# PSUM banks handed on to other tiles, a new order of the first products, and dense dummy products during the loads, in a gated mix of linear attention and SwiGLU

## The chip, the cores and the metric

The kernel runs on one core of one Trainium2 chip. The metric is the time of one execution in microseconds (us), taken on the device. Every time quoted is of a fast run; no run in this study was of the slow state. The engines are called as the profile calls them: PE (TensorE), DVE (VectorE), ACT (ScalarE), POOL (GpSimd), SP (SyncE, which here only issues transfers).

## The reference, cut to what matters

```python
x = A_x                                           # 1 x 2048 x 512, bf16
g = sigmoid((x * gate_w).sum(-1, keepdims=True))
# A: linear attention, 32 heads of 16
q, k, v = split(x @ wqkv)
pq, pk = phi(q), phi(k)                           # phi(t) = where(t > 0, t + 1, exp(t)) + 1e-6
kv  = einsum("bhsd,bhse->bhde", pk, v)            # sums over ALL tokens
z   = einsum("bhsd->bhd", pk)
a   = (einsum(pq, kv) / (einsum(pq, z) + 1e-6)) @ wo
# B: SwiGLU
b   = (silu(x @ w1) * (x @ w3)) @ w2              # F = 1376
return g * a + (1 - g) * b
```

The sums over all tokens come first. The kernel does not form v: it accumulates XP = x^T pk over the 16 token tiles of 128 tokens in four PSUM banks (XP0 to XP3), and multiplies by the weights of v afterwards. So the program begins with: load x and the key weights, transpose x, k = x wk, pk = phi(k), XP += x^T pk.

## The kernel before

The kernel keeps eight buffers in PSUM, each of up to 128 x 512 fp32, which are called banks here. Four (`psM`, tag "mm") rotate. The other four belong to three pools one after another: first the keys of token tiles 0 to 3, then the XP accumulators, then two output and two query buffers.

```python
psM = tile_pool(name="psM", bufs=4, space=PSUM)
...
def phi(dst, ps):                                 # one key or query tile, 128 x 512
    e  = exp(ps)                                  # ACT
    em = min(e, 1.0) + 1e-6                       # DVE, phi_m
    dst = max(ps, 0.0) + em                       # DVE, the last reader of the bank
...
warm = psM.tile([P, P], FP32, tag="mm", name="warm")
for i in range(18):                               # 18 dummy products of 128 columns
    nc.tensor.matmul(warm[:], lhsT=zeros[:], rhs=zeros[:], start=True, stop=True)
mask_ps = psM.tile([P, P], FP32, tag="mm", name="mask_ps")
nc.tensor.matmul(mask_ps[:], lhsT=EhT[:], rhs=EhT[:], start=True, stop=True)
nc.vector.tensor_copy(out=blockmask[:], in_=mask_ps[:])
...
def emit_xT(t):                                   # transposes token tile t on PE
    xTp = psM.tile([P, KC, P], BF16, tag="mm", name="xTp")
    ...                                           # 4 transposes, then a copy by DVE or ACT
...
with tc.tile_pool(name="psE", bufs=1, space=PSUM) as psE:
    k0 = [psE.tile([P, D], FP32, tag=f"k{t}", name=f"k0_{t}") for t in range(TPB)]
    emit_xT(0)
    emit_k_mm(k0[0], 0, 0)                        # key tile 0, contraction chunk 0 of 4
    emit_xT(1)
    emit_k_mm(k0[0], 0, 1)
    emit_k_mm(k0[1], 1, 0)
    emit_xT(2)
    ...                                           # the rest, then the last chunk of each:
    for t in range(TPB):
        emit_k_mm(k0[t], t, 3)
        emit_k_phi(k0[t], t)

with tc.tile_pool(name="psX", bufs=1, space=PSUM) as psX:      # the four banks of psE again
    XP_ps = [psX.tile([P, D], FP32, tag=f"XP{dc}", name=f"XP{dc}") for dc in range(KC)]
    for t in range(TPB, NT):
        emit_k(t)                                 # 4 products, bank from psM
        emit_xp(...)                              # 4 products, one into each XP bank
    ...
psO = tile_pool(name="psO", bufs=2, space=PSUM)   # and these again the same four
psQ = tile_pool(name="psQ", bufs=2, space=PSUM)
```

The order of instructions on PE is the order of the program; the other engines are ordered by the framework.

Of the kernel before, what the change touches and what calls it, by code (L numbers as in the profile page):

```python
# [8 lines left out]
ACT = mybir.ActivationFunctionType  # L9
# [3 lines left out]
FP32 = mybir.dt.float32  # L13
BF16 = mybir.dt.bfloat16
# [3 lines left out]
def kernel(  # L18
# [12 lines left out]
    nc = tc.nc  # L31
    P = nc.NUM_PARTITIONS

    Bb, S, D = A_x.shape
# [3 lines left out]
    KC = D // P  # L38
    NT = S // P
    TB = 512  # L40
    NTB = S // TB
    TPB = TB // P
# [9 lines left out]
    consts = ctx.enter_context(tc.tile_pool(name="consts", bufs=1))  # L52
    work = ctx.enter_context(tc.tile_pool(name="work", bufs=3))
    blk = ctx.enter_context(tc.tile_pool(name="blk", bufs=2))
    psM = ctx.enter_context(tc.tile_pool(name="psM", bufs=4, space=bass.MemoryType.PSUM))


    zeros = consts.tile([P, P], BF16, name="zeros")
    nc.vector.memset(zeros[:], 0.0)
    ident = consts.tile([P, P], BF16, name="ident")  # L60
    make_identity(nc, ident[:])
# [3 lines left out]
        out=EhT[:], in_=EhT[:], pattern=[[1, P]], compare_op=ALU.is_ge, fill=0.0,  # L65
# [3 lines left out]
        out=EhT[:], in_=EhT[:], pattern=[[-1, P]], compare_op=ALU.is_ge, fill=0.0,  # L69
# [32 lines left out]
    for tb in range(1, NTB):  # L102
        dq.dma_start(
            out=xT[:, :, tb * TB : (tb + 1) * TB], in_=x2d[tb * TB : (tb + 1) * TB, :],
# [3 lines left out]
            out=x_sb[:, tb * TPB : (tb + 1) * TPB, :], in_=x_r[:, tb * TPB : (tb + 1) * TPB, :]  # L108
# [4 lines left out]
    with nc.allow_non_contiguous_dma(reason="one gate weight per partition and chunk"):  # L113
        dq.dma_start(
            out=wr_sb[:, :, 2 * FR : NR], in_=gate_w.rearrange("(kc d o) -> d kc o", d=P, o=1)
# [11 lines left out]
    XP_sb = consts.tile([P, KC, D], BF16, name="XP_sb")  # L127
# [22 lines left out]
    ctx.enter_context(tc.manual_schedule(engines={ENG.PE}))  # L150


    warm = psM.tile([P, P], FP32, tag="mm", name="warm")
    for i in range(18):
        nc.tensor.matmul(warm[:], lhsT=zeros[:], rhs=zeros[:], start=True, stop=True)
    mask_ps = psM.tile([P, P], FP32, tag="mm", name="mask_ps")
    nc.tensor.matmul(mask_ps[:], lhsT=EhT[:], rhs=EhT[:], start=True, stop=True)
    nc.vector.tensor_copy(out=blockmask[:], in_=mask_ps[:])

    st = {}  # L160

    def emit_xT(t):
        xTp = psM.tile([P, KC, P], BF16, tag="mm", name="xTp")
        for kc in range(KC):
            nc.tensor.transpose(
                out=xTp[:, kc, :], in_=x_sb[:, t, kc * P : (kc + 1) * P], identity=ident[:]
            )
        xT_t = xT[:, :, t * P : (t + 1) * P]
        if t % 2 == 0:
            nc.vector.tensor_copy(out=xT_t, in_=xTp[:])  # L170
        else:
            nc.scalar.activation(out=xT_t, in_=xTp[:], func=ACT.Copy)

    def emit_k_mm(k_ps, t, kc):
        nc.tensor.matmul(  # L175
            k_ps[:], lhsT=xT[:, kc, t * P : (t + 1) * P], rhs=wk_sb[:, kc, :],
            start=(kc == 0), stop=(kc == KC - 1),
        )

    def emit_k_phi(k_ps, t):  # L180
        e_ins = phi(pk_sb[:, t, :], k_ps[:])
        if t == 0:
            nc.gpsimd.tensor_copy(pks[:], pk_sb[:, t, :])
        else:
            nc.gpsimd.tensor_add(pks[:], pks[:], pk_sb[:, t, :])  # L185

    def emit_k(t):
        k_ps = psM.tile([P, D], FP32, tag="mm", name="k_ps")
        for kc in range(KC):
            emit_k_mm(k_ps, t, kc)  # L190
        emit_k_phi(k_ps, t)

    def emit_xp(t, XP_ps):
        for dc in range(KC):
            nc.tensor.matmul(  # L195
                XP_ps[dc][:], lhsT=x_sb[:, t, dc * P : (dc + 1) * P], rhs=pk_sb[:, t, :],
                start=(t == 0), stop=(t == NT - 1),
            )

    def emit_q(tb, tt, pool, tag):  # L200
        t = tb * TPB + tt
        ts_tok = slice(t * P, (t + 1) * P)
        if tt == 0:
            st[tb, "pq"] = blk.tile([P, TPB, D], BF16, tag="pq", name="pq")
            st[tb, "den"] = blk.tile([P, TPB, H], FP32, tag="den", name="den")
        q_ps = pool.tile([P, D], FP32, tag=tag, name="q_ps")
        for kc in range(KC):
            nc.tensor.matmul(  # L208
                q_ps[:], lhsT=xT[:, kc, ts_tok], rhs=wq_sb[:, kc, :],
                start=(kc == 0), stop=(kc == KC - 1),  # L210
            )
        phi(st[tb, "pq"][:, tt, :], q_ps[:])
# [105 lines left out]
    def emit_out(tb, tt):  # L318
        t = tb * TPB + tt
        tsl = slice(tt * P, (tt + 1) * P)  # L320
        o_ps = psO.tile([P, D], FP32, tag="o", name="o_ps")
        for c in range(KC):
            nc.tensor.matmul(  # L323
                o_ps[:], lhsT=st[tb, "pqT"][:, c, tsl], rhs=W_sb[:, c, :],
                start=(c == 0), stop=False,
            )
        nc.tensor.matmul(  # L327
            o_ps[:], lhsT=st[tb, "hTr"][:FR, tsl], rhs=w2r_sb[:FR, :], start=False, stop=False
        )
        for fc in range(FC):  # L330
            nc.tensor.matmul(  # L331
                o_ps[:], lhsT=st[tb, "hT"][:, fc, tsl], rhs=w2_sb[:, fc, :],
                start=False, stop=(fc == FC - 1),
            )
        o_out = work.tile([P, D], BF16, tag="o_out", name="o_out")
        nc.scalar.activation(  # L336
            out=o_out[:], in_=o_ps[:], func=ACT.Copy, scale=omg[:, t : t + 1]
        )
        nc.sync.dma_start(out=out2d[t * P : (t + 1) * P, :], in_=o_out[:])


    with tc.tile_pool(name="psE", bufs=1, space=bass.MemoryType.PSUM) as psE:
        k0 = [psE.tile([P, D], FP32, tag=f"k{t}", name=f"k0_{t}") for t in range(TPB)]
        emit_xT(0)
        emit_k_mm(k0[0], 0, 0)
        emit_xT(1)
        emit_k_mm(k0[0], 0, 1)
        emit_k_mm(k0[1], 1, 0)
        emit_xT(2)
        emit_k_mm(k0[1], 1, 1)  # L350
        emit_k_mm(k0[0], 0, 2)
        emit_k_mm(k0[1], 1, 2)
        emit_xT(3)
        for kc in range(KC - 1):
            emit_k_mm(k0[2], 2, kc)
        for kc in range(KC - 1):
            emit_k_mm(k0[3], 3, kc)
        for t in range(TPB):
            emit_k_mm(k0[t], t, 3)
            emit_k_phi(k0[t], t)  # L360


    with tc.tile_pool(name="psX", bufs=1, space=bass.MemoryType.PSUM) as psX:
        XP_ps = [psX.tile([P, D], FP32, tag=f"XP{dc}", name=f"XP{dc}") for dc in range(KC)]
        n_xp = 0
        for t in range(TPB, NT):
            emit_k(t)
            for u in range(n_xp, n_xp + (2 if t in (NT - 4, NT - 2) else 1)):
                emit_xp(u, XP_ps)
                n_xp = u + 1  # L370
        emit_q(0, 0, psM, "mm")
        emit_xp(NT - 2, XP_ps)
        emit_q(0, 1, psM, "mm")
        emit_xp(NT - 1, XP_ps)
        for dc in range(KC):
            if dc % 2 == 0:
                nc.scalar.activation(out=XP_sb[:, dc, :], in_=XP_ps[dc][:], func=ACT.Copy)
            else:
                nc.vector.tensor_copy(out=XP_sb[:, dc, :], in_=XP_ps[dc][:])

    psO = ctx.enter_context(tc.tile_pool(name="psO", bufs=2, space=bass.MemoryType.PSUM))
    psQ = ctx.enter_context(tc.tile_pool(name="psQ", bufs=2, space=bass.MemoryType.PSUM))

    emit_q(0, 2, psM, "mm")
    emit_q(0, 3, psM, "mm")
    emit_rem(0, 0, psM, "mm")
    emit_rem(0, 1, psM, "mm")
    kvT_ps = psQ.tile([P, KC, P], FP32, tag="q", name="kvT_ps")
    for c in range(KC):
        csl = slice(c * P, (c + 1) * P)  # L390
        for dc in range(KC):
            nc.tensor.matmul(
                kvT_ps[:, c, :], lhsT=wv_sb[:, dc, csl], rhs=XP_sb[:, dc, csl],
                start=(dc == 0), stop=(dc == KC - 1),
# [2 lines left out]
        out=kvT_sb[:], in0=kvT_ps[:],  # L397
        in1=blockmask[:, None, :].to_broadcast([P, KC, P]), op=ALU.mult,
    )
    z_ps = psQ.tile([P, D], FP32, tag="q", name="z_ps")  # L400
    nc.tensor.matmul(z_ps[:], lhsT=ones_f[:], rhs=pks[:], start=True, stop=True)
    nc.scalar.activation(out=z_sb[:], in_=z_ps[:], func=ACT.Copy)
    for fc in range(FC):
        emit_ffn(0, fc)
        if 1 <= fc <= TPB:
            emit_den(0, fc - 1)
        if fc == TPB + 1:
            emit_norm(0)
        if fc in (1, 3):
            for c in range(fc - 1, fc + 1):  # L410
                W_ps = psQ.tile([P, D], FP32, tag="q", name="W_ps")
                nc.tensor.matmul(
                    W_ps[:], lhsT=kvT_sb[:, c, :], rhs=wo_sb[:, c, :], start=True, stop=True
                )
                nc.scalar.activation(out=W_sb[:, c, :], in_=W_ps[:], func=ACT.Copy, scale=2.0)

    for tb in range(NTB):
        for fc in range(FC if tb == 0 else 0, FC):
            emit_ffn(tb, fc)
        nx = tb + 1  # L420
        for tt in range(TPB):
            if nx < NTB:
                emit_q(nx, tt, psQ, "q")
                if tt % 2 == 0:
                    emit_rem(nx, tt // 2, psQ, "q")
            emit_out(tb, tt)
            if nx < NTB:
                emit_den(nx, tt)
        if nx < NTB:
            emit_norm(nx)  # L430
# [30 lines left out]
```

## Time and profile before

| | before |
|---|---|
| time, median of the first three runs (range) | 190.68 us (189.19 to 191.50) |
| span of the profiled run | 188.4 us |
| PE busy | 178.1 us, 95% |
| longest wait of PE | 3.9 us, XP for pk_sb |
| half clock recorded after that wait | 3.4 us |

The lines are in the prediction below. Three habits of reading are needed. The rows of 40 slices show where an engine isn't full; only there can PE gain. A wait names the instruction that ended it, and the reader must ask whether that instruction is needed for its data or only because it frees a buffer. And the granted clock is read beside the waits: in the trace of before, products of 512 columns start 0.43 us apart at half clock (427 ns) and 0.22 us apart at full clock (216 ns).

### The profile page before, as it was taken

What the parts mean: (1) busy time and instruction counts of PE and PEld (TensorE: products, weight loads), DVE (VectorE), ACT (ScalarE), POOL (GpSimd) and SP (SyncE); (2) the same over time, 40 slices, a digit from 0 to 9 for tenths busy, and PEclk for the clock granted to TensorE, in tenths of its full rate; (3) what the DMA queues carried; (4) which work ended last, traced back from release to release, by engine and by line L of the source; (5) the groups of instructions that cost most, each with busy time, mean ns of one, the idle gap of its engine ahead of it and who ended that gap; (6) DMA issues with size and microseconds to landing.
All of it is one profiled execution on the core that took longest, in us unless ns stands there. A gap on an engine that the chain in (4) does not pass through costs nothing.

```text
span 188.4 us, 2440 instructions
## 1 busy us (share of the span) xinstructions
PE 178.1 (95%) x873; PEld 84.5 (45%) x873; DVE 117.8 (63%) x204; ACT 66.0 (35%) x123; POOL 59.4 (32%) x67
## 2 busy tenths in 40 slices
PE   6865999999999999999999999999999999999991
PEld 5421444447444454544445454444454544444440
DVE  2055578569699893649787646787883659875000
ACT  3160333228463323433334333433333432331211
POOL 4019375640834432326200333460032327100000
PEclk9996999999999999999999999999999999999998
DMA  5999999600100501012400010141001112300010
GB/s 164 217 285 210 298 391 369 192 0 0 24 11 0 110 1 45 28 44 56 84 0 3 14 56 14 56 87 31 0 0 42 35 38 67 72 0 0 31 56 30
DMA packets 28189, 14.88 MB, mean 79 GB/s; under 512 B 19632, under 2 KB 27152, under 8 KB 28176
## 3 DMA queue, kind: packets, MB, share of 16 engines
q1 hardware_dynamic: 27744, 14.33, 28.4%
q10 hardware_dynamic: 432, 0.39, 0.6%
q8 instruction: 7, 0.11, 0.2%
q14 instruction: 6, 0.05, 0.1%
HBM read 8.42 MB, written 2.10 MB: 56 GB/s over the span
## 4 chain that ended last, share of the span: by engine, by line
PE 92%; DMA 2%; DVE 2%; ACT 1%; issue 0%; SPq 0%; ACTq 0%
PE up_ps L304 18%; PE o_ps L331 18%; PE gate_ps L298 18%; PE q_ps L208 7%; PE o_ps L323 7%; PE k_ps L175 5%; PE r_ps L232 3%; DMA wk_sb<-in_A_wqkv_dram 2%; PE XP_228 L195 2%; PE XP_230 L195 2%; PE XP_229 L195 2%; PE XP_231 L195 2%; PE o_ps L327 2%; DVE phi_m L142 1%; DVE pk_sb L145 1%; PE k_1_157 L175 1%
## 5 line engine op out<-in xcount | busy, mean ns | idle before, releaser
L298 PE MATMUL gate_ps<-xT,w_sb 128*128 128x512 bf16 x160 | 41.1, 379 | 0.0
L304 PE MATMUL up_ps<-xT,w_sb 128*128 128x512 bf16 x160 | 41.0, 379 | 0.0
L309 ACT ACTIVATE th<-gate_ps 128x512 bf16<-128x512 f32 x40 | 23.9, 597 | 39.1 <-PE gate_ps L298 38.7
L216 POOL TENSOR_TENSOR qz<-pq,z_sb 128x512 f32<-128x512 bf16 x16 | 18.5, 1162 | 59.7 <-DVE pq L145 58.9
L331 PE MATMUL o_ps<-w_sb,hT 128*128 128x512 bf16 x160 | 37.1, 379 | 0.0
L142 DVE TENSOR_SCALAR phi_m<-phi_e 128x512 bf16<-128x512 bf16 x32 | 14.2, 447 | 27.6 <-ACT phi_e L140 27.6
L311 DVE SCALAR_TENSOR_TENSOR gs<-th,gate_ps 128x512 bf16<-128x512 bf16 x40 | 27.4, 684 | 6.0 <-ACT th L309 5.8
L314 DVE TENSOR_TENSOR hT<-up_ps,gs 128x512 bf16<-128x512 f32 x40 | 27.6, 690 | 3.7
L298 PEld LDWEIGHTS <-w_sb 128*128 128x128 bf16 x160 | 15.6, 98 | 19.2 <-issue 0.6
L304 PEld LDWEIGHTS <-w_sb 128*128 128x128 bf16 x160 | 15.6, 98 | 19.0 <-issue 0.2
L331 PEld LDWEIGHTS <-hT 128*128 128x128 bf16 x160 | 15.6, 98 | 19.0
L336 ACT ACTIVATE o_out<-o_ps,omg 128x512 bf16<-128x512 f32 x16 | 11.0, 688 | 31.7 <-PE o_ps L331 31.7
L281 POOL TENSOR_TENSOR pqn<-pq,rden 128x512 bf16<-128x512 bf16 x16 | 16.6, 1057 | 15.3 <-DVE rden L274 12.9
L185 POOL TENSOR_TENSOR pks<-pks,pk_sb 128x512 f32<-128x512 f32 x15 | 17.5, 1164 | 10.9 <-DVE pk_sb L145 10.5
L219 DVE TENSOR_REDUCE den<-qz 128x32 f32<-128x512 f32 x16 | 10.9, 684 | 9.4 <-POOL qz L216 9.4
L323 PE MATMUL o_ps<-W_sb,pqT 128*128 128x512 bf16 x64 | 16.4, 379 | 0.0
L208 PE MATMUL q_ps<-wq_sb,xT 128*128 128x512 bf16 x64 | 16.3, 379 | 0.0
L140 ACT ACTIVATE phi_e<-k_ps 128x512 bf16<-128x512 f32 x12 | 7.2, 598 | 19.2 <-PE k_ps L175 17.0
L175 PE MATMUL k_ps<-wk_sb,xT 128*128 128x512 bf16 x48 | 12.9, 394 | 0.0
L140 ACT ACTIVATE phi_e<-q_ps 128x512 bf16<-128x512 f32 x16 | 9.6, 597 | 7.8 <-PE q_ps L208 7.8
L195 PEld LDWEIGHTS <-x_sb 128*128 128x128 bf16 x64 | 6.3, 100 | 12.2 <-DVE pk_sb L145 4.4
L145 DVE SCALAR_TENSOR_TENSOR pq<-q_ps,phi_m 128x512 bf16<-128x512 f32 x16 | 11.1, 691 | 0.5
(74 smaller groups left out, 139.7 us busy)
## 6 DMA issues: line engine op xcount, KB each, us to landing
w_sb<-in_B_w_dram SPq DMA_DIRECT2D x3, 1280.0 KB, 10.9
out_dram<-o_out SPq DMA_DIRECT2D x16, 128.0 KB, 1.7
x_sb<-in_A_x_dram SPq DMA_DIRECT2D x3, 512.0 KB, 4.5
wk_sb<-in_A_wqkv_dram SPq DMA_DIRECT2D x4, 128.0 KB, 4.2
wq_sb<-in_A_wqkv_dram SPq DMA_DIRECT2D x1, 512.0 KB, 5.5
wv_sb<-in_A_wqkv_dram SPq DMA_DIRECT2D x1, 512.0 KB, 5.4
wo_sb<-in_A_wo_dram SPq DMA_DIRECT2D x1, 512.0 KB, 11.9
x_sb<-in_A_x_dram ACTq DMA_DIRECT2D x3, 128.0 KB, 3.0
```

The costliest lines, as they stand in the source:

```text
L175: nc.tensor.matmul(k_ps[:], lhsT=xT[:, kc, t * P : (t + 1) * P], rhs=wk_sb[:, kc, :], start=(kc == 0), stop=(kc == KC - 1),)
L185: nc.gpsimd.tensor_add(pks[:], pks[:], pk_sb[:, t, :])
L195: nc.tensor.matmul(XP_ps[dc][:], lhsT=x_sb[:, t, dc * P : (dc + 1) * P], rhs=pk_sb[:, t, :], start=(t == 0), stop=(t == NT - 1),)
L208: nc.tensor.matmul(q_ps[:], lhsT=xT[:, kc, ts_tok], rhs=wq_sb[:, kc, :], start=(kc == 0), stop=(kc == KC - 1),)
L216: nc.gpsimd.tensor_tensor(out=qz[:], in0=st[tb, "pq"][:, tt, :], in1=z_sb[:], op=ALU.mult)
L298: nc.tensor.matmul(gate_ps[:], lhsT=w1_sb[:, kc, fsl], rhs=xT[:, kc, tok_sl], start=(kc == 0), stop=(kc == KC - 1),)
L304: nc.tensor.matmul(up_ps[:], lhsT=w3_sb[:, kc, fsl], rhs=xT[:, kc, tok_sl], start=(kc == 0), stop=(kc == KC - 1),)
L309: nc.scalar.activation(out=th[:], in_=gate_ps[:], func=ACT.Tanh, scale=0.5)
L311: nc.vector.scalar_tensor_tensor(out=gs[:], in0=th[:], scalar=1.0, in1=gate_ps[:], op0=ALU.add, op1=ALU.mult)
L314: nc.vector.tensor_tensor(out=st[tb, "hT"][:, fc, :], in0=up_ps[:], in1=gs[:], op=ALU.mult)
L323: nc.tensor.matmul(o_ps[:], lhsT=st[tb, "pqT"][:, c, tsl], rhs=W_sb[:, c, :], start=(c == 0), stop=False,)
L331: nc.tensor.matmul(o_ps[:], lhsT=st[tb, "hT"][:, fc, tsl], rhs=w2_sb[:, fc, :], start=False, stop=(fc == FC - 1),)
```

## The change

Its intent is to let PE pass from the first keys to the XP accumulation without waiting for the last of the first four keys to be read, and to keep PE dense while loads land, from which the author expected that its clock is raised early. The diff, cut to its core:

```diff
-    zeros = consts.tile([P, P], BF16, name="zeros")
+    zeros = consts.tile([P, TB], BF16, name="zeros")
...
+    psX = ctx.enter_context(tc.tile_pool(name="psX", bufs=1, space=bass.MemoryType.PSUM))
+    def emit_warm(n, cols):
+        warm = psX.tile([P, TB], FP32, tag="XP2", name="warm")
+        ...                                       # n dummy products of cols columns
+    emit_warm(5, TB)                              # instead of 18 of 128 columns
-    mask_ps = psM.tile([P, P], FP32, tag="mm", name="mask_ps")
+    mask_ps = psX.tile([P, P], FP32, tag="XP0", name="mask_ps")
...
-        xTp = psM.tile([P, KC, P], BF16, tag="mm", name="xTp")
+        xTp = psX.tile([P, KC, P], BF16, tag=f"XP{t % 3}", name="xTp")
...
-        o_ps = psO.tile([P, D], FP32, tag="o", name="o_ps")
+        o_ps = psX.tile([P, D], FP32, tag=f"XP{2 + tt % 2}", name="o_ps")
...
-    with tc.tile_pool(name="psE", bufs=1, ...) as psE:
-        k0 = [psE.tile([P, D], FP32, tag=f"k{t}", name=f"k0_{t}") for t in range(TPB)]
-        emit_xT(0); emit_k_mm(k0[0], 0, 0); emit_xT(1); emit_k_mm(k0[0], 0, 1)
-        emit_k_mm(k0[1], 1, 0); emit_xT(2); ...
+    k0 = [psX.tile([P, D], FP32, tag="XP3", name="k0_0")]
+    k0 += [psM.tile([P, D], FP32, tag="mm", name=f"k0_{t}") for t in range(1, TPB)]
+    emit_xT(0); emit_warm(4, P); emit_xT(1); emit_k_mm(k0[0], 0, 0); emit_warm(2, P)
+    emit_xT(2); emit_k_mm(k0[0], 0, 1); emit_k_mm(k0[1], 1, 0); emit_k_mm(k0[1], 1, 1)
+    emit_xT(3); ...
+    emit_k_mm(k0[0], 0, 3); emit_k_phi(k0[0], 0)  # key 0's last chunk now before key 3
+    ...
+    emit_warm(6, P)
...
     for t in range(TPB, NT):
-        emit_k(t)
-        ...emit_xp...
+        ...emit_xp...
+        emit_k(t)
...
-                emit_q(nx, tt, psQ, "q")
+                emit_q(nx, tt, psX, "XP0")
```

(The lines with semicolons stand for one call per line; kvT_ps, z_ps, W_ps and the remainder tiles move from psQ to XP banks in the same way. `t % 2 == 0` in emit_xT became `t in (0, 2)`; it is called for tiles 0 to 3 only, so that does nothing.)

More of the change, by code (lines that the diff above doesn't have):

```diff
@@ L150 @@
     ctx.enter_context(tc.manual_schedule(engines={ENG.PE}))
-    warm = psM.tile([P, P], FP32, tag="mm", name="warm")
-    for i in range(18):
-        nc.tensor.matmul(warm[:], lhsT=zeros[:], rhs=zeros[:], start=True, stop=True)
-    mask_ps = psM.tile([P, P], FP32, tag="mm", name="mask_ps")
+    psX = ctx.enter_context(tc.tile_pool(name="psX", bufs=1, space=bass.MemoryType.PSUM))
+    def emit_warm(n, cols):
+        warm = psX.tile([P, TB], FP32, tag="XP2", name="warm")
+        for i in range(n):
+            nc.tensor.matmul(
+                warm[:, 0:cols], lhsT=zeros[:, 0:P], rhs=zeros[:, 0:cols], start=True, stop=True
+            )
+    emit_warm(5, TB)
+    mask_ps = psX.tile([P, P], FP32, tag="XP0", name="mask_ps")
     nc.tensor.matmul(mask_ps[:], lhsT=EhT[:], rhs=EhT[:], start=True, stop=True)
@@ L168, in emit_xT @@
         xT_t = xT[:, :, t * P : (t + 1) * P]
-        if t % 2 == 0:
+        if t in (0, 2):
             nc.vector.tensor_copy(out=xT_t, in_=xTp[:])
@@ L339, in emit_out @@
         nc.sync.dma_start(out=out2d[t * P : (t + 1) * P, :], in_=o_out[:])
-    with tc.tile_pool(name="psE", bufs=1, space=bass.MemoryType.PSUM) as psE:
-        k0 = [psE.tile([P, D], FP32, tag=f"k{t}", name=f"k0_{t}") for t in range(TPB)]
-        emit_xT(0)
-        emit_k_mm(k0[0], 0, 0)
-        emit_xT(1)
-        emit_k_mm(k0[0], 0, 1)
-        emit_k_mm(k0[1], 1, 0)
-        emit_xT(2)
-        emit_k_mm(k0[1], 1, 1)
-        emit_k_mm(k0[0], 0, 2)
-        emit_k_mm(k0[1], 1, 2)
-        emit_xT(3)
-        for kc in range(KC - 1):
-            emit_k_mm(k0[2], 2, kc)
-        for kc in range(KC - 1):
-            emit_k_mm(k0[3], 3, kc)
-        for t in range(TPB):
-            emit_k_mm(k0[t], t, 3)
-            emit_k_phi(k0[t], t)
@@ L363 @@
-    with tc.tile_pool(name="psX", bufs=1, space=bass.MemoryType.PSUM) as psX:
-        XP_ps = [psX.tile([P, D], FP32, tag=f"XP{dc}", name=f"XP{dc}") for dc in range(KC)]
-        n_xp = 0
-        for t in range(TPB, NT):
-            emit_k(t)
-            for u in range(n_xp, n_xp + (2 if t in (NT - 4, NT - 2) else 1)):
-                emit_xp(u, XP_ps)
-                n_xp = u + 1
-        emit_q(0, 0, psM, "mm")
-        emit_xp(NT - 2, XP_ps)
-        emit_q(0, 1, psM, "mm")
-        emit_xp(NT - 1, XP_ps)
-        for dc in range(KC):
-            if dc % 2 == 0:
-                nc.scalar.activation(out=XP_sb[:, dc, :], in_=XP_ps[dc][:], func=ACT.Copy)
-            else:
-                nc.vector.tensor_copy(out=XP_sb[:, dc, :], in_=XP_ps[dc][:])
@@ L381 @@
-    psO = ctx.enter_context(tc.tile_pool(name="psO", bufs=2, space=bass.MemoryType.PSUM))
-    psQ = ctx.enter_context(tc.tile_pool(name="psQ", bufs=2, space=bass.MemoryType.PSUM))
+    k0 = [psX.tile([P, D], FP32, tag="XP3", name="k0_0")]
+    k0 += [psM.tile([P, D], FP32, tag="mm", name=f"k0_{t}") for t in range(1, TPB)]
+    emit_xT(0)
+    emit_warm(4, P)
+    emit_xT(1)
+    emit_k_mm(k0[0], 0, 0)
+    emit_warm(2, P)
+    emit_xT(2)
+    emit_k_mm(k0[0], 0, 1)
+    emit_k_mm(k0[1], 1, 0)
@@ new lines @@
+    emit_k_mm(k0[1], 1, 1)
+    emit_xT(3)
+    emit_k_mm(k0[0], 0, 2)
+    emit_k_mm(k0[1], 1, 2)
+    for kc in range(KC - 1):
+        emit_k_mm(k0[2], 2, kc)
+    emit_k_mm(k0[0], 0, 3)
+    emit_k_phi(k0[0], 0)
+    for kc in range(KC - 1):
+        emit_k_mm(k0[3], 3, kc)
+    for t in range(1, TPB):
+        emit_k_mm(k0[t], t, 3)
+        emit_k_phi(k0[t], t)
+    emit_warm(6, P)
+    XP_ps = [psX.tile([P, D], FP32, tag=f"XP{dc}", name=f"XP{dc}") for dc in range(KC)]
+    n_xp = 0
+    for t in range(TPB, NT):
+        for u in range(n_xp, n_xp + (2 if t in (NT - 4, NT - 1) else 1)):
+            emit_xp(u, XP_ps)
+            n_xp = u + 1
+        emit_k(t)
@@ L384 @@
+    emit_q(0, 0, psM, "mm")
+    emit_xp(NT - 2, XP_ps)
+    emit_q(0, 1, psM, "mm")
+    emit_xp(NT - 1, XP_ps)
+    for dc in range(KC):
+        if dc % 2 == 0:
+            nc.scalar.activation(out=XP_sb[:, dc, :], in_=XP_ps[dc][:], func=ACT.Copy)
+        else:
+            nc.vector.tensor_copy(out=XP_sb[:, dc, :], in_=XP_ps[dc][:])
     emit_q(0, 2, psM, "mm")
@@ L387 @@
     emit_rem(0, 1, psM, "mm")
-    kvT_ps = psQ.tile([P, KC, P], FP32, tag="q", name="kvT_ps")
+    kvT_ps = psX.tile([P, KC, P], FP32, tag="XP0", name="kvT_ps")
     for c in range(KC):
@@ L399 @@
     )
-    z_ps = psQ.tile([P, D], FP32, tag="q", name="z_ps")
+    z_ps = psX.tile([P, D], FP32, tag="XP1", name="z_ps")
     nc.tensor.matmul(z_ps[:], lhsT=ones_f[:], rhs=pks[:], start=True, stop=True)
@@ L410 @@
             for c in range(fc - 1, fc + 1):
-                W_ps = psQ.tile([P, D], FP32, tag="q", name="W_ps")
+                W_ps = psX.tile([P, D], FP32, tag=f"XP{c}", name="W_ps")
                 nc.tensor.matmul(
@@ L422 @@
             if nx < NTB:
-                emit_q(nx, tt, psQ, "q")
+                emit_q(nx, tt, psX, "XP0")
                 if tt % 2 == 0:
-                    emit_rem(nx, tt // 2, psQ, "q")
+                    emit_rem(nx, tt // 2, psX, "XP1")
             emit_out(tb, tt)
```

## The prediction

> **What bounds the kernel now.** I read the page first. The engine rows and the 40 slices say that TensorE (PE) is the bound nearly everywhere:
>
> ```profile
> span 188.4 us, 2440 instructions
> PE 178.1 (95%) x873; PEld 84.5 (45%) x873; DVE 117.8 (63%) x204; ACT 66.0 (35%) x123; POOL 59.4 (32%) x67
> ...
> PE   6865999999999999999999999999999999999991
> ...
> PEclk9996999999999999999999999999999999999998
> ```
>
> A slice is 188.4/40 = 4.71 us. From slice 5 to slice 39 PE is at 90% or more, so after about 19 us only less PE work could help. What can be had lies in the first four slices, and slice 3 (14.1 to 18.8 us) also shows the granted clock at 0.6. The waits of PE name what stands there:
>
> ```profile
> PE XP_228 L195 <- DVE pk_sb L145: 3.9, 1, 3.9
> PE warm L155 <- DVE zeros L59: 1.1, 1, 1.1
> PE k_0_156 L175 <- DMA wk_sb<-in_A_wqkv_dram: 0.7, 1, 0.7
> PE k_0_156 L175 <- DVE xT L170: 0.5, 1, 0.5
> ```
>
> These are all its waits: one of 3.9 us, and two short ones while the loads land. The windows by stage (columns: length, busy time of PE, PEld, DVE, ACT, POOL, then the granted clock) show what the long one does to the clock:
>
> ```profile
> 15.40:15.80 0.40, 0.00 (x0) 0.00 (x0) 0.40 (x3) 0.00 (x0) 0.34 (x1) 1.00 1.16 248
> 15.80:16.20 0.40, 0.00 (x0) 0.00 (x0) 0.40 (x1) 0.00 (x0) 0.40 (x1) 0.62 1.29 292
> 16.20:18.80 2.60, 2.41 (x6) 0.89 (x7) 0.73 (x2) 0.00 (x0) 2.44 (x3) 0.50 0.89 240
> 18.80:19.20 0.40, 0.40 (x2) 0.15 (x1) 0.00 (x0) 0.00 (x0) 0.40 (x1) 0.50 1.02 361
> 19.20:19.60 0.40, 0.40 (x3) 0.14 (x2) 0.00 (x0) 0.00 (x0) 0.01 (x1) 0.87 1.07 379
> ```
>
> At 0.5 or 1 as the only levels, 0.62 means the drop came at 15.90 and 0.87 that the clock was back at 19.30: 3.4 us of half clock, just after the gap. Last, the timeline of PE and DVE around the gap:
>
> ```profile
> 8.65 0.59 PE L165 MATMUL xTp<-ident,x_sb 128*128 128x128 bf16 x4
> 9.08 0.81 PE L175 MATMUL k_2_158<-wk_sb,xT 128*128 128x512 bf16 x3
> ...
> 10.59 0.38 PE L175 MATMUL k_0_156<-wk_sb,xT 128*128 128x512 bf16 x1
> ...
> 16.39 0.61 PE L195 MATMUL XP_228<-pk_sb,x_sb 128*128 128x512 bf16 x1 [3.91 <-DVE pk_sb L145]
> ```
>
> ```profile
> 11.96 0.69 DVE L145 SCALAR_TENSOR_TENSOR pk_sb<-k_0_156,phi_m 128x512 bf16<-128x512 f32 x1
> ...
> 15.66 0.68 DVE L145 SCALAR_TENSOR_TENSOR pk_sb<-k_3_159,phi_m 128x512 bf16<-128x512 f32 x1
> ```
>
> The first XP product needs, as data, only pk_sb of token tile 0, which DVE finished at 11.96 + 0.69 = 12.65. It started at 16.39, right after pk_sb of tile 3 (15.66 + 0.68 = 16.34). So 3.7 us of the gap is no data dependence but a bank one: the XP accumulators take the banks of the first four keys, and the wait is for the last of them to be read. Starts of 512-column products are 0.43 us apart up to 9.08 and 0.22 after it, so the clock was half until then, although the page's clock row, which seems to lack the state before its first event, shows 1.00 there.
>
> [...] half clock for 19.30 - 15.90 = 3.40 us, and steps back from 15.90 by 3.41 give 12.49, 9.08, 5.67 and 2.26; 9.08 is exactly the first fast product, and 12.49 to 15.90 was wholly idle. [...]
>
> **The change part by part.**
>
> Banks. XP0 to XP2 now follow the transposes (tile t in XP0, XP1, XP2, XP0) and XP3 follows key 0. The transposes are copied out long before; key 0's last reader is pk_sb of tile 0, which the first XP product needs anyway. The gap shrinks to the true dependence. Keys 1 to 3 go to the rotating four, where key tiles 5 to 7 wait for them. DVE finished pk_sb 1, 2 and 3 1.4, 2.0 and 3.7 us after pk_sb 0; the pace on PE is one XP group plus one key group, 8 x 0.216 = 1.73 us. Tile 1 is wanted 1.73 us after tile 0, tile 2 3.46 and tile 3 5.19. No wait in the loop.
>
> Order. Key 0's last product moves up by the three of key 3 (3 x 0.216 = 0.65 us). In the loop XP comes before the key, one tile nearer to its producer: three tiles, some 5 us, against a chain of 0.60 (ACT) + 0.3 to 1.2 + 0.69 (DVE) = 1.6 to 2.5 us. Enough.
>
> Dummies. Eighteen 128-column products at 0.107 us (1.92 us) become five of 512 at 0.427 (2.13): +0.21. The zeros are four times as large; from the two early memsets (0.11 us for 64 words, 0.17 for 128, about 1 ns a word) 256 words take 0.30: +0.2. Four and two of 128 columns (0.43 + 0.21 us at half clock) fall in the 0.5 and 0.7 us waits before the second and third step; six at the end (0.33 us at full clock) in the rest of the gap.
>
> A new wait. The mask and the transpose of tile 0 now share XP0. The mask copy on DVE took 0.29 us and would end at about 3.97, so the first transpose starts at about 4.0, not 3.31: 0.7 us later. It delays a part that waits for weights until 6.10 anyway.
>
> After the loop. q takes XP0 alone and the remainder XP1, where two buffers rotated. In the first output stage q products start at 66.00, 70.79, 74.89 and 79.68 and their pq ends at 68.71, 73.50, 77.61: the next comes 1.3 to 2.1 us later. W, z and kvT likewise. No cost, no gain; that PE work is unchanged.
>
> The sum, on PE's clock. Before: XP of tile 0 starts at 16.39 with key 4 done, and the half clock to 19.30 costs (19.30 - 16.39)/2 = 1.45, so a full-clock start at 17.84. After, worked by hand:
> A, full clock from 9.08 as now: first transposes 4.0 to 4.43, dummies to 4.86, transpose 1 to 5.29, key 0 to 5.72, dummies to 5.93, transpose 2 to 6.36; then five 0.43 steps and transpose 3 to about 8.9; three products of key 2, then key 0's last starts at 9.7. From that start to pk_sb 0 took 12.65 - 10.59 = 2.06 us, so XP starts at 11.8. Key 4 (0.86) is still to do: equivalent 12.66. Saving 17.84 - 12.66 = 5.2 us.
> B, full clock from 5.67: after the weights at 6.10 all goes at 0.22; key 0's last product starts at about 8.1, XP at 10.2, equivalent 11.06. Saving 6.8 us.
> Which? By streaming time, window 2.26 to 5.67 was 61% busy (36% without transposes) and did not release the clock; 5.67 to 9.08 was 86% (63%) and did. After the change the first of these has 2.9 of 3.4 us, 84% (59%). That is near the one that did; I give B 6 in 10. Expected saving 0.6 x 6.8 + 0.4 x 5.2 = 6.1 us.
>
> **The rivals.** First, DVE takes the place of the bank: with the gap gone, pk_sb for tiles 1 to 3 and then one tile every 1.73 us must keep up, while phi_m stretches to 1.2 us beside POOL's 1.16 us adds. For it: DVE is busy 100% from 12.4 to 16.4. Against: part of that is backlog of five tiles arriving in a burst, and in the loop it still idles 0.3 to 3.5 us before most tiles. It would return 1 to 2 us: 186.
> Second, loads become the bound, as all is wanted 5 to 7 us sooner. For it: the queues are full until about 36 us. Against: the transposed tokens of tiles 8 and 12 were issued at 7.40 and 11.43 and land about 5.6 us later, 13.0 and 17.0, while their keys now come at about 18 and 25. The load of wq is issued after the last x at 15.5, lands in 5.5, and is wanted at 33. Under 0.5 us.
> Third, the clock phase decides. The three times before, 189.19 to 191.50, spread 2.3 us, about what a window's phase can do twice. [...] after the change the first full-clock moment still varies by up to a window, worth half of it. It moves single runs by 1 to 1.5 us, either way.
>
> **Range and chances.** 190.68 - 6.1 = 184.6 us. A with some DVE waiting and a lucky before gives 186.4; B with a slow before gives 183.0. Faster by over 2% means below 186.87, so a saving of 3.8 us; the bank gap alone, without its clock, is about that. I give 0.94. Slower would need a new wait of 10 us, of which I see no sign.
>
> **What would show it.** The gap before the first XP at under 0.8 us, released by pk_sb of tile 0; no clock under 1.00 after the first fast product; first XP between 10 and 12 us; the first transpose at about 4.0 after the mask copy; slices from there on all 9 for PE, and stages after the loop of the same lengths, shifted. It is wrong if XP of tiles 1 to 3 waits for pk_sb, if PE cools in a new gap, or if q_ps waits for DVE in the output stages.

## The result, and the profile after

The changed kernel took 183.74 us (median of four runs, 182.58 to 184.86) against 190.69 us. The ratio is 0.964, 95% interval 0.956 to 0.973. A ratio is the mean time of one kernel's fast runs over that of the other's of the same rounds, so it isn't quite the ratio of the medians.

The page of the changed kernel, the same lines as were shown of before:

```profile
span 182.0 us, 2418 instructions
PE 175.8 (97%) x855; PEld 84.0 (46%) x872; DVE 117.3 (64%) x204; ACT 66.3 (36%) x123; POOL 59.6 (33%) x67
...
PE   6999999999999999999999999999999999999992
...
PEclk9999999999999999999999999999999999999999
```

PE is full from the second slice on, and the dent of the clock in slice 3 is gone. (Busy time fell by 2.3 us; some records of products are missing in this trace, 855 against 873, so that number is not used.) These are all the waits of PE that are left (columns: in total, times, longest):

```profile
PE warm L158 <- DVE zeros L59: 1.3, 1, 1.3
PE xTp L172 <- DVE blockmask L165: 0.4, 1, 0.4
```

The 3.9 us are gone, the two short waits during the loads too (dummy products stand in their place), and one new wait of 0.4 us stands at the start: transpose 0 now shares a bank with the mask, whose copy must be finished. The timeline of PE and of DVE where the gap was:

```profile
10.62 0.50 PE L158 MATMUL warm<-zeros 128*128 128x128 bf16 x6
11.23 0.39 PE L202 MATMUL XP_226<-pk_sb,x_sb 128*128 128x512 bf16 x1
...
12.10 1.03 PE L182 MATMUL k_ps<-wk_sb,xT 128*128 128x512 bf16 x4
```

```profile
10.48 0.69 DVE L145 SCALAR_TENSOR_TENSOR pk_sb<-k_0_143,phi_m 128x512 bf16<-128x512 f32 x1
...
13.02 0.68 DVE L145 SCALAR_TENSOR_TENSOR pk_sb<-k_3_146,phi_m 128x512 bf16<-128x512 f32 x1
```

The first XP product starts at 11.23, right after pk_sb of tile 0 (10.48 + 0.69 = 11.17), and 2.5 us before pk_sb of tile 3 is done. Where the time went is read by comparing two moments of both kernels. First the first gate product, from the chain of before and of after:

```profile
47.92 0.86 PE gate_ps L298 x4
...
184.37 0.69 ACT o_out L336
```

```profile
42.21 0.22 PE gate_ps L305
...
178.55 0.69 ACT o_out L343
```

Before the gate products 5.7 us were saved; between them and the last evacuation, o_out, both kernels take the same within 0.1 us (136.45 and 136.34). The span fell by 6.4 us, so 0.6 us were also saved after the last evacuation. That part the prediction did not have. The transfer view of the last 3.4 us before the end, before and after, shows it:

```profile
q14 instruction: 1, 0.01, 1.3%
issues: line engine op xcount, KB each, median us to landing
out_dram<-o_out SPq DMA_DIRECT2D x1, 128.0 KB, 2.5
```

```profile
out_dram<-o_out SPq DMA_DIRECT2D x1, 128.0 KB, 1.7
```

In the kernel before, one packet of an instruction queue moves while the last store does, and that store takes 2.5 us to land instead of 1.7. The packets in the trace itself show how the two are linked: 135 of the store's 144 packets have started by 186.43 us, the instruction packet runs from 186.10 to 186.83, and the last nine start at 186.82 and are done at 187.17. In the changed kernel the instruction packet moves too, but at 182.31, 0.3 us after the end of the span.

### The profile page after: what moved, and what is told of

Same layout as the page of the kernel before. It is cut to its first block, busy times and chain, and to the rows that moved or that the text cites. A ratio compares the mean times of both kernels' runs of the same rounds, so it can differ in the third digit from the quotient of the medians.

```text
span 182.0 us, 2418 instructions
## 1 busy us (share of the span) xinstructions
PE 175.8 (97%) x855; PEld 84.0 (46%) x872; DVE 117.3 (64%) x204; ACT 66.3 (36%) x123; POOL 59.6 (33%) x67
## 4 chain that ended last, share of the span: by engine, by line
PE 96%; DVE 1%; issue 1%; ACT 1%; ACTq 0%
PE gate_ps L305 19%; PE o_ps L338 19%; PE up_ps L311 19%; PE q_ps L215 8%; PE o_ps L330 7%; PE k_ps L182 6%; PE r_ps L239 3%; PE o_ps L334 2%; PE XP_226 L202 2%; PE XP_228 L202 2%; PE XP_227 L202 2%; PE XP_229 L202 2%; PE warm L158 2%; PE xTp L172 1%; PE k_0_143 L182 1%
## 5 line engine op out<-in xcount | busy, mean ns | idle before, releaser
L311 PE MATMUL up_ps<-xT,w_sb 128*128 128x512 bf16 x156 | 40.5, 379 | 0.1
L142 DVE TENSOR_SCALAR phi_m<-phi_e 128x512 bf16<-128x512 bf16 x32 | 13.3, 419 | 22.7 <-ACT phi_e L140 22.5
L182 PE MATMUL k_ps<-wk_sb,xT 128*128 128x512 bf16 x47 | 12.3, 379 | 0.1
L215 PEld LDWEIGHTS <-xT 128*128 128x128 bf16 x64 | 6.3, 98 | 7.5
```

Of the source, the lines that this page charges most:

```text
L182: nc.tensor.matmul(k_ps[:], lhsT=xT[:, kc, t * P : (t + 1) * P], rhs=wk_sb[:, kc, :], start=(kc == 0), stop=(kc == KC - 1),)
L215: nc.tensor.matmul(q_ps[:], lhsT=xT[:, kc, ts_tok], rhs=wq_sb[:, kc, :], start=(kc == 0), stop=(kc == KC - 1),)
L311: nc.tensor.matmul(up_ps[:], lhsT=w3_sb[:, kc, fsl], rhs=xT[:, kc, tok_sl], start=(kc == 0), stop=(kc == KC - 1),)
```

## The experiments

My theory was the bank theory: the gain is the bank wait (3.7 us without need in the data) and the half clock that follows an idle gap. The first rival was that the dense dummies make the gain, by raising and keeping the clock; the second that the new order does; the third that the free phase of the clock window, not the kernel, moves single runs. (In the traces the granted clock, after its first rise, changes at whole multiples of 3.41 us from it: after 2, 3 and 52 of them in before, after 51 in the changed kernel, after 3 and 4 in f2. One such step is called a window here, and where a run begins within it is its phase.) All twelve kernels gave correct outputs. Four earlier runs, e0 to e3, with the edits of f0 to f3, found no chip and gave no result. The diffs are cut: the width of `zeros` goes with the dummies, and helper code is left out.

| run | what differs | median us | ratio to before (95%) |
|---|---|---|---|
| f0_after_again | the changed kernel again | 183.61 | 0.9643 (0.9608 to 0.9679) |
| f1_no_dummies | changed, without new dummies | 183.41 | 0.9636 (0.9588 to 0.9684) |
| f2_dummies_only | before, with dense dummies | 189.30 | 0.9952 (0.9928 to 0.9976) |
| f3_gap_filled | before, gap filled with dummies | 188.30 | 0.9892 (0.9861 to 0.9923) |
| g1_xp3_after_key3 | changed, one bank swapped back | 186.63 | 0.9777 (0.9738 to 0.9815) |
| g2_key0_late | changed, key 0's last product late | 185.18 | 0.9692 (0.9641 to 0.9742) |
| g3_key_first | changed, key 4 before the first XP | 184.16 | 0.9635 (0.9601 to 0.9668) |
| g4_combined | g3, mask later, denser dummies | 182.46 | 0.9553 (0.9523 to 0.9583) |
| h1_combined_no_dummies | g4 without dummies | 182.03 | 0.9596 (0.9545 to 0.9648) |
| h2_banks_alone | before, only the banks changed | 184.92 | 0.9711 (0.9682 to 0.9741) |
| h3_transposed_dummies | g4, dummies are transposes | 182.34 | 0.9568 (0.9535 to 0.9600) |
| i1_prologue_order | h2 with the new early order | 183.70 | 0.9634 (0.9603 to 0.9665) |

The four f runs shared one chip, the four g and three h runs another, i1 a third; before ran on each (190.35, 190.90, 190.61 and 190.63 us in the four batches).

### f0_after_again: the same kernel in another phase

No edit.

> The changed kernel once more, for more free phases of the clock window. Bank theory: first XP product between 10.2 and 11.8 us, released by pk_sb of tile 0, no half clock after the first fast product; 182.5 to 185 us. The moment of the first fast product should differ from the 7.8 us of the first trace, by up to one window of 3.4 us, if the window runs freely.

Measured: the ratio repeats. The profiled run, 184.97 us, came late: the trace's clock record has the first full clock at 10.24 us, against 7.62 us in the first trace, and the first XP starts at 12.51 instead of 11.23, outside the range that was expected. Clock 2.62 us later, XP 1.28 us later: half of it, as it should be when PE is dense and works at half speed until then. So the phase differs from run to run, by amounts that matter here.

### f1_no_dummies: banks and order without dummies

```diff
-    emit_warm(5, TB)
+    emit_warm(18, P)
...
-    emit_warm(4, P)
-    emit_warm(2, P)
-    emit_warm(6, P)
```

> The banks and the order of the change, without its dense dummies (18 short ones at the start as before). Bank theory: most of the gain stays, since 3.7 us of wait and 1.45 us of half clock go with the bank; first XP at 11 to 12.5 us, 184 to 185.5 us, ratio to before 0.967 to 0.972. Rival theory, that the dummies make the gain by keeping the clock up: without them only the bare wait of 3.7 us or less is won, some half clock appears again, 187 us or more.

Measured: 0.9636, the whole gain, and more than the 0.967 to 0.972 expected. The dummies add nothing that can be told here. The profiled run even was the earliest in its full clock of all (4.53 us), so its first XP came at 9.97 us; that is one phase, and its six runs, from 182.28 to 184.86 us, do not let it be called a merit of the edit.

### f2_dummies_only: the dummies without the banks

```diff
-    for i in range(18):
-        nc.tensor.matmul(warm[:], lhsT=zeros[:], rhs=zeros[:], start=True, stop=True)
+    emit_warm(5, TB)                  # into a psM tile
...
         emit_xT(0)
+        emit_warm(4, P)
...
         emit_xT(1)
+        emit_warm(2, P)
```

> The kernel before with the dense dummies alone (five of 512 columns, then four and two of 128), banks and order as before. Bank theory: the wait of 3.9 us for pk_sb of tile 3 stays and the half clock after it may stay; at most 1 us won by an earlier full clock, 189.5 to 190.7 us, ratio 0.993 to 1.0. Rival theory, dummies: 186 us or less.

Measured: 0.9952, so 0.9 us won, the interval clear of 1. The bank wait stays, in the timeline of PE, and in the windows (where the granted clock is the third number from the end, 0.51) so does the half clock:

```profile
15.20 1.04 PE L200 MATMUL XP<-pk_sb,x_sb 128*128 128x512 bf16 x3 [3.92 <-DVE pk_sb L145]
```

```profile
16.20:19.60 3.40, 3.40 (x10) 1.21 (x8) 0.98 (x2) 0.60 (x1) 1.74 (x2) 0.51 0.94 299
```

The clock record has half clock from 16.29 to 19.70, after XP had begun at 15.20. The window of 3.41 us that ends at 16.29 was not idle: PE had worked from 15.20 on, 1.09 us or 32% of it, and the clock still fell. All 3.41 us of half clock are then lost work, 1.7 us, more than the 1.45 of the first trace. The rival that the dummies make the gain is out: f1 and f2 say it from both sides.

### f3_gap_filled: what the half clock alone costs

```diff
             emit_k(t)
+            if t == TPB:
+                emit_warm(17, TB)
```

> The kernel before with 17 dummy products of 512 columns (17 x 0.216 = 3.7 us at full clock) put into the wait before the first XP product; the bank wait itself stays. If the half clock behind the gap costs what I worked out (1.45 us, when a whole window falls into the gap), the first XP still starts at about 16.4 us, the granted clock stays 1.00 to 20 us, and the time falls by 0.7 to 1.45 us, ratio 0.992 to 0.996. If the half clock had another cause than the idle gap, it stays and the time is that of before. If the phase keeps the array slow until after 12 us, the dummies themselves are slow and push the first XP later.

Measured: 0.9892, or 2.05 us (interval 1.5 to 2.6), more than the 0.7 to 1.45 expected. The timeline of PE shows that XP starts no earlier:

```profile
12.57 3.83 PE L156 MATMUL warm<-zeros 128*128 128x512 bf16 x17
16.65 0.60 PE L200 MATMUL XP<-pk_sb,x_sb 128*128 128x512 bf16 x2 [0.25 <-DVE pk_sb L145]
```

Yet no half clock is recorded between 10.22 us and the end. So the half clock behind the gap is caused by the gap, and is worth some 2 us. Nor is any run of before spared it: the granted clock listed with each of the 49 runs of before is 0.991 or lower, at least 1.7 us of the span lost, while the six of f3 list 0.997 or more. It also shows why 1.45 us was too little. Twelve of the 49 list 0.981 or 0.982, a loss of 3.4 to 3.6 us. The profiled run lost 1.7 us in its one window and 0.9 us at the end; by estimate these twelve lost two windows behind the gap.

### g1_xp3_after_key3: one bank swapped back

```diff
-    k0 = [psX.tile([P, D], FP32, tag="XP3", name="k0_0")]
-    k0 += [psM.tile([P, D], FP32, tag="mm", name=f"k0_{t}") for t in range(1, TPB)]
+    k0 = [psM.tile([P, D], FP32, tag="mm", name=f"k0_{t}") for t in range(TPB - 1)]
+    k0 += [psX.tile([P, D], FP32, tag="XP3", name="k0_3")]
```

> The changed kernel with one bank swapped back: the fourth XP accumulator follows key tile 3 instead of key tile 0. All dummies and the order stay. Bank theory: the first three XP products start on pk_sb of tile 0, the fourth waits for pk_sb of tile 3, which came 2.5 us later in the changed kernel (13.70 against 11.17), so PE gets a wait of about 1.9 us (2.53 less the three products' 0.65) released by DVE pk_sb, and the time rises by 1.5 to 2.2 us, to about 185.5, ratio 0.972 to 0.977. Rival theories, order or dummies: no change, ratio 0.964.

Measured: the predicted wait is there, in the timeline of PE, at the fourth XP product:

```profile
12.29 0.82 PE L202 MATMUL XP<-pk_sb,x_sb 128*128 128x512 bf16 x3
14.81 0.38 PE L202 MATMUL XP<-pk_sb,x_sb 128*128 128x512 bf16 x1 [1.70 <-DVE pk_sb L145]
```

The ratio is 0.9777. Against f0 that is (0.9777 - 0.9643) x 190.9 = 2.6 us, above the 1.5 to 2.2 expected and above the 1.70 us in the trace; the profiled run of g1 has no half clock after the wait. The slowest of its four runs (187.17 us) lists a granted clock of 0.989 where the others list 0.997 to 1.000, so by estimate it lost one window's half clock to this shorter wait, which is part of the excess. The same data, the same order, the same dummies: one bank alone sets this wait. This is the direct proof of the bank theory.

### g2_key0_late: key 0's last product back in its old place

```diff
-    emit_k_mm(k0[0], 0, 3)
-    emit_k_phi(k0[0], 0)
     for kc in range(KC - 1):
         emit_k_mm(k0[3], 3, kc)
-    for t in range(1, TPB):
+    for t in range(TPB):
```

> The changed kernel with the last product of key 0 put back behind the three of key 3, so pk_sb of tile 0 comes about 0.65 us later. Bank theory with order as a small part: wait before the first XP grows by 0.65 us less nothing, time up by 0.4 to 0.7 us, ratio 0.966 to 0.969, hard to tell from the spread of single runs (2 us); the trace should show a wait of 0.6 to 1.0 us before the first XP. Rival theory, that the order makes the gain: 187 us or more.

Measured: a wait of 0.76 us before the first XP, as expected. With its first full clock at 10.02 us it is to be compared with f0 (10.24 us): XP at 13.05 against 12.51, though its clock came earlier by 0.22 us, worth 0.11. That is 0.65 us, exactly the three products moved. The times (0.9692, some 0.9 us slower) agree within their intervals.

### g3_key_first: real work in place of the last dummies

```diff
-    emit_warm(6, P)
...
     for t in range(TPB, NT):
+        emit_k(t)
         for u in ...:
             emit_xp(u, XP_ps)
-        emit_k(t)
```

> The changed kernel with key 4 in front of the first XP group, in place of the last six dummies, and the loop in the order of before (key, then XP). The wait for pk_sb of tile 0 (0.33 us of dummies and 0.28 us idle in the changed kernel) is then filled by 0.86 us of real work: 0.6 us won, ratio 0.960 to 0.962, first XP with key 4 done at most 0.3 us later than without. If DVE falls behind (first rival of the prediction), XP of tile 1 waits for pk_sb instead and nothing is won.

Measured: 0.9635 where 0.960 to 0.962 was expected; the gain can't be told from none by the times. The trace shows it: no wait is left before XP (10.81, 0.86 us of key 4, then XP at 11.68):

```profile
10.81 1.03 PE L182 MATMUL k_ps<-wk_sb,xT 128*128 128x512 bf16 x4
11.68 1.03 PE L202 MATMUL XP<-pk_sb,x_sb 128*128 128x512 bf16 x4
```

At its phase (8.03 us) the changed kernel would stand at 12.09 + 0.49 x 0.41 = 12.29 with key 4 paid; g3 is there at 11.68, 0.6 us earlier. That the spread of the phase hides this in six runs is argued, not shown.

### g4_combined and h1_combined_no_dummies: dummies against the phase

g4 adds to g3 (h1 is g4 with 18 short dummies at the start and none later):

```diff
-    mask_ps = psX.tile(... tag="XP0" ...)    # and its product and copy, at the start
...
     for t in range(TPB, NT):
+        if t == 2 * TPB:
+            mask_ps = psM.tile(... tag="mm" ...)    # product and copy here
...
     emit_xT(0)
-    emit_warm(4, P)
+    emit_warm(8, P)
     emit_xT(1)
     emit_k_mm(k0[0], 0, 0)
-    emit_warm(2, P)
     emit_xT(2)
+    emit_warm(4, P, "XP0")
```

> g3 and besides: the mask product moved from the start into the key loop, so that no PE wait for its copy is left at the start, and eight and four dummies in the two load waits, so that PE never stands still for more than 0.2 us before 7 us. Phase theory: any window of 3.4 us that begins after 1.2 us is then busy above 85%, so the full clock comes between 4.5 and 7.7 us in every run, and the spread of the times shrinks to about 1.5 us; 182.0 to 183.0 us, ratio 0.955 to 0.962. If the phase is not what spreads the runs, the spread stays near 2.3 us.

> g4 without its dummies: eighteen short ones at the start as in the kernel before, none later. Phase theory: the load waits leave some windows of 3.4 us under the share that releases the clock, so the full clock comes anywhere from 4.5 to 10 us; single runs spread over 2 us again (0.6 us in g4) and the mean is 0.3 to 1.0 us slower than g4, ratio 0.957 to 0.961. Rival: the dummies are worth nothing in any arrangement and the gain of g4 over g3 is the moved mask alone; then ratio 0.955 and spread as g4.

Measured, all single runs:

```
g4: 182.48 181.94 182.51 181.94 182.44 182.55
h1: 184.38 184.60 181.92 181.90 181.95 182.10
```

The spread of g4 is 0.6 us, that of h1 2.7 us. h1 falls into two groups: the profiled run, with the full clock at 10.10 us, is one of the slow two. The fastest runs of both are equal. So denser dummies do not make the fast case faster; they would keep the slow case from happening. None of g4's six runs and two of h1's are slow, which chance could give, so this is likely, not shown. In the mean g4 is ahead by 0.4%, with overlapping intervals, so that isn't shown either. Against the changed kernel (0.9643) g4 is ahead by 0.9%, intervals disjoint: it beats both kernels.

### h2_banks_alone and i1_prologue_order: what the banks alone give, and the early order

h2 is the kernel before with the banks of the change and nothing else: old dummies, old order everywhere. i1 adds the new order of the first transposes and key products:

```diff
     emit_xT(0)
-    emit_k_mm(k0[0], 0, 0)
     emit_xT(1)
+    emit_k_mm(k0[0], 0, 0)
+    emit_xT(2)
     emit_k_mm(k0[0], 0, 1)
     emit_k_mm(k0[1], 1, 0)
-    emit_xT(2)
     emit_k_mm(k0[1], 1, 1)
+    emit_xT(3)
     emit_k_mm(k0[0], 0, 2)
     emit_k_mm(k0[1], 1, 2)
-    emit_xT(3)
```

> The kernel before with nothing but the banks changed: no new dummies, every order on PE as before (key 0's last product late, key 4 in front of the first XP). Bank theory: the wait of 3.9 us for pk_sb of tile 3 becomes one for pk_sb of tile 0, which key 4 (0.86 us) covers but for about 0.3 us; no half clock after it; ratio 0.962 to 0.968, so all of the change's 6.8 us within 0.5 us. If order or dummies had a real share, 0.972 or more.

> h2 (banks alone, 0.971) with one thing more: the order of the first transposes and key products as in the change (tile 1 is transposed right after tile 0 instead of behind the first key product, and both steps of key 1 come before transpose 3). No dummies, key 0's last product late, key 4 in front of the first XP. If that order is what h2 lacks against f1 (0.9636), because PE no longer stands for 0.5 us behind the copy of tile 0 and the windows fill earlier, the ratio is 0.961 to 0.966. If h2 lacks the early last product of key 0 instead, it stays at 0.969 to 0.972.

Measured: h2 0.9711, outside the 0.962 to 0.968 that the bank theory expected and short of the 0.972 of its rivals; i1 0.9634, the intervals disjoint. So the banks alone are 2.9% of the 3.6%, and the early order another 0.8% (1.5 us). i1 has the whole gain without the new dummies and with key 0 late. The timelines of PE show what the early order does. In h2 the first key product stands between the transposes and waits for the copy of tile 0:

```profile
3.75 0.58 PE L172 MATMUL xTp<-ident,x_sb 128*128 128x128 bf16 x4 [0.38 <-DVE blockmask L165]
4.86 0.61 PE L182 MATMUL k<-wk_sb,xT 128*128 128x512 bf16 x1 [0.52 <-DVE xT L177]
```

In i1 tile 1 is transposed in that time:

```profile
3.75 1.01 PE L172 MATMUL xTp<-ident,x_sb 128*128 128x128 bf16 x8 [0.38 <-DVE blockmask L165]
4.86 0.61 PE L182 MATMUL k<-wk_sb,xT 128*128 128x512 bf16 x1
...
12.66 1.02 PE L182 MATMUL k_ps<-wk_sb,xT 128*128 128x512 bf16 x4 [0.38 <-DVE pk_sb L145]
```

The last line shows something else. With key 4 in front and key 0 late, key 5 waits 0.38 us for pk_sb of tile 1, whose bank it takes: the prediction's first rival, DVE behind, in a small form. In the changed kernel it does not occur.

At equal phase h2 is behind i1 by 0.7 us (by the table below: 12.94 less 11.62, less half of the 1.31 us that its clock came later). The rest of the 1.5 us would be that waits on PE leave more phases in which the clock rises late; that is argued, not shown.

### h3_transposed_dummies: do transposes count as activity?

```diff
-            nc.tensor.matmul(warm[:, 0:cols], lhsT=zeros[:, 0:P], rhs=zeros[:, 0:cols], ...)
+            nc.tensor.transpose(out=warm[:, 0:P], in_=zeros[:, 0:P], identity=ident[:])
```

> g4 with every dummy product replaced by 128-column transposes of zeros of the same streaming time (20, 8 and 4 of them). If transposes count as PE activity for the clock, as the shares of the windows in the traces so far suggest, the full clock comes between 4.5 and 8 us as in g4 and the time is that of g4 within 0.7 us (they start some 0.3 us later, when the identity is ready), ratio 0.955 to 0.959. If they do not count, no window before 6 us can release the clock, it comes at 9 to 12 us, and the time is 184 us or more, ratio 0.964 or more.

Measured: 0.9568 and a spread of 1.0 us, near g4's 0.9553 and 0.6 us; the clock record has full clock at 6.36 us. The timeline of PE shows key products 0.22 us apart right behind the transposes (three within 0.81 us, each modelled at 0.38).

```profile
4.03 1.06 PE L158 MATMUL warm<-ident,zeros 128*128 128x128 bf16 x8
...
6.16 0.49 PE L158 MATMUL warm<-ident,zeros 128*128 128x128 bf16 x4
6.48 0.81 PE L177 MATMUL k<-wk_sb,xT 128*128 128x512 bf16 x3
```

Before 6.36 PE had done one key product of 0.43 us; all else in the window from 2.95 to 6.36 was transposes. So in this trace the transposes counted as activity for the clock; whether in full isn't shown.

### All traces in one table

F is the first full clock by the trace's clock record (for the dip of before it has 15.89 to 19.31 us, where the prediction read 15.90 to 19.30 from the windows). S is the start of the first XP group as if key 4 were done: plus 0.86 us where key 4 comes after it, plus the later 0.38 us wait in h2 and i1; in g1 the end of the interrupted XP group; plus the work lost to a later half clock in before (1.45) and f2 (1.71).

```
run      F us    S us    time us   time - S
before   9.07   17.84    190.17    172.3
f2       6.04   16.91    189.51    172.6
f3      10.22   16.65    189.09    172.4
after    7.62   12.09    183.71    171.6
f0      10.24   13.37    184.97    171.6
f1       4.53   10.83    182.54    171.7
g1       9.79   15.02    186.62    171.6
g2      10.02   13.91    185.71    171.8
g3       8.03   11.68    183.26    171.6
g4       6.20   10.62    182.48    171.9
h1      10.10   12.53    184.38    171.9
h2       8.70   12.94    184.73    171.8
h3       6.36   10.81    182.68    171.9
i1       7.39   11.62    183.56    171.9
```

The last column is constant within 0.4 us in each family. So everything but one step is decided by the first 18 us, and that step, 0.7 us in the mean between the family with the old pools and the one with the new, is the end: from the start of the last evacuation to the end of the span it is 4.02, 4.40 and 4.21 us in the first three, and 3.43 to 3.46 us in the eleven others. In each of the first three a packet of instruction queue q14 moves within the last 3.4 us and the last store lands after 2.5 to 2.7 us; its last nine packets start only where that packet ends (186.82, 185.95 and 185.67 us). In the eleven others no q14 packet moves in these 3.4 us (in the changed kernel it comes at 182.31, 0.3 us after the end of the span), and the store lands after 1.7. Why it comes earlier in the old pools' program was not tested: h2 has as many instructions on PE as before, so it is not their number on PE.

## Why the prediction was right or wrong

**The bank wait: right.** It was read as a wait with no data behind it, and g1 brings it back with one bank. The first XP is released by pk_sb of tile 0 as said, and no later XP waits in the changed kernel.

**The half clock behind the gap: right in kind, too small in size.** 1.45 us were taken from one trace; f3 gives 2.05 (1.5 to 2.6), f2 shows a case of 1.71, and a quarter of the runs of before seem to lose two windows. A gap without a whole idle window costs it too: in f2 a window with 32% of work lost the clock, and no run of before was spared.

**The dummies: the step that failed.** The prediction put scenario B, full clock from 5.67 us, at 6 in 10 because the dummies would fill the window from 2.26 to 5.67, and took 1.6 us for it. It took the window's phase from the trace of before as if it were fixed. The clock came at 7.62 and 10.24 us in two traces of the changed kernel, and without the dummies the ratio is the same (0.9636 against 0.9643). The prediction saw the free phase, but only as a spread around its two cases. The kernel's own start leaves windows that don't suffice: PE begins at 1.26 us instead of 1.06 and waits 0.38 us for the mask, and windows of 66 to 78% of work there did not raise the clock. By streaming time at half clock (0.107 us for 128 columns, the spacing of the short dummies in the trace of before), windows of 58% (h1), 61% (before), 66% (after), 73% (f0) and 78% (g3) did not raise it; windows of 80% (f1), 85% (f2), 86% (before) and 92% (after) did. So in these traces the share needed lies near four fifths, an estimate: the shares are good to a per cent or two. A sum slipped as well: +0.21 and +0.2 us put the end of the mask copy at 4.11, not 3.97; it came at 4.12. Whether the dummies gain in some phases what they lose in others isn't shown; in g4, filled more densely, none of six runs was late.

**The order: mis-sized.** The prediction priced key 0's move (0.65 us, exactly what g2 shows) but gave no worth to the new order of the first transposes and key products (tile 1 transposed right behind tile 0 above all); h2 and i1 give that 1.5 us.

**The end: missing.** The earlier end of the last store gives 0.6 us in the two first traces and 0.8 in the mean of all, and no step had it.

**Why the sum still held.** 6.1 us were expected, 6.8 measured (3.57% of 190.35). Saving A, 5.2 us, was mostly the banks, and h2 measures 5.5 us, of which some 0.6 is the end. The expected further 0.9 us for the clock was wrong in its cause, but the early order stood in for it. The number was good in part by compensation.

**The rivals.** DVE as the new bound shows only in h2 and i1, where key 5 waits 0.38 us. The late loads never were one. In the changed kernel PE has no wait for a load at all, because dummies stand there; without them it waits 0.44 us (f1) and 0.95 us (h1) for the key weights. The phase as a source of spread was right, and larger than said: 2.7 us in h1.

## What to carry to other kernels

When a wait names the last reader of a buffer, ask whether its data are needed. If not, give the new tile the buffers whose readers are done earliest, above all for the accumulators that start a long dense stretch. And where the time of single runs spreads by a per cent or more, look for the clock's first rise in the traces before believing small differences. Dense dummies must be measured by themselves: those of the change brought nothing that could be told from noise beside the banks, and 0.5% in the old kernel.
